# Two tables that fix the issue sequence of five queues in a top-32 attention, FFN and Sinkhorn MoE kernel

## The chip, the cores and the metric

One core of a Trainium2 chip runs the whole program. The metric is device time in microseconds; a kernel's time is the median of its runs. The engines are PE (TensorE, matrix products and transposes), DVE (VectorE), ACT (ScalarE), POOL (GpSimd) and SP (SyncE, whose queue issues the DMAs). Each engine works through one queue of its own in the order in which the program lists its instructions, and waits on semaphores for the others.

## The reference

All data are float32. Attention takes q, k, v of 2 batches x 8 heads x 576 positions x 64; then come a dense FFN and a mixture of 8 experts that are all evaluated for all 1152 tokens.

```python
scores = scale * np.matmul(q, k.transpose(0, 1, 3, 2))
kth = np.partition(scores, -top_k, axis=-1)[..., -top_k:-top_k + 1]   # top_k = 32
scores = np.where(scores >= kth, scores, -1e9)
attn = np.exp(scores - np.max(scores, axis=-1, keepdims=True))
attn = attn / (np.sum(attn, axis=-1, keepdims=True) + 1e-09)
x = np.matmul(attn, v)                        # put together to 1152 x 512
h = x @ w_in                                  # 512 x 2048
x = (h * (1.0 / (1.0 + np.exp(-h)))) @ w_out  # 2048 x 512
logits = x @ w_gate
P = np.exp(logits - logits.max())             # 1152 x 8
for _ in range(8):
    P /= P.sum(1, keepdims=True) + 1e-09
    P /= P.sum(0, keepdims=True) + 1e-09
    P *= N / E
for e in range(E):                            # w1[e] 512 x 1024, w2[e] 1024 x 512
    out += P[:, e:e + 1] * (np.maximum(x @ w1[e], 0.0) @ w2[e])
```

## The kernel before

Most products are split: each operand becomes a high and a low part in the format fp32r, and `mm3` (L145 to L147) issues three matmuls for one. `split` (L135, L136) and `evac_split` (L139, L140) make the parts: ACT copies the high part, and POOL or DVE subtracts.

**Attention** (to about 500 us) goes in five groups g = 0 to 4 of query rows, over four head pairs each. `score_tile` handles a tile of 128 rows x 576 columns: PE makes the scores (L320), ACT copies them to `s` (L323), and DVE finds the 32 largest of each row in four rounds: a MAX (L333) takes the next eight into `m8`, and between two rounds a MATCH_REPLACE (L340) strikes these eight out, writing the copy `w`, which the next MAX reads. ACT has meanwhile made the exponentials `e`; one SCALAR_TENSOR_TENSOR (L343) masks them with the 32nd largest value and sums the row, a RECIPROCAL (L346) follows, ACT scales the tile (L348), PE transposes it (L351, L354) and multiplies it by v (`av`, L370). So the seven MAX and MATCH_REPLACE of one tile and its L343 each need the result of the one ahead. There are 64 such tiles, with up to three of them under way on DVE at a time.

**Beside it** PE gets other work: the first token tile's FFN (`first_row`), experts for that tile (`row_ffn`, with `gr_e` on ACT at L658), and the FFN of group g (`m1` to `m4`, names `g_m`, `gH_m`, `gL_m`) once the group's attention `xH`, `xL` is there. From 500 us on come `m4`, expert 0 for the last four token tiles (`e0_5`), and, in between, the gate logits and six of the eight Sinkhorn iterations (`iteration`, L912 to L921): in each of them DVE makes column sums `cs` (L917), PE adds them over the partitions with a small matmul `pm_c` (L906), and DVE goes on from its result. From about 644 us on experts 7 to 1 follow (products `h`, `yA`, `yB`), in which PE works almost without a break.

**What sets the order.** The program is traced in source order; a scheduler then sorts each engine's instructions by priorities (`tc.cur_priority`, set all over the kernel) and by its own estimate of when they could run, with a few hand-written constraints (`tc.issue_after`). Buffers of a pool are shared by tiles with the same tag, in the order in which the schedule comes to the tiles.

## Time and profile before

| | |
|---|---|
| time, median of 3 runs | 1222.95 us (1221.66 to 1225.37) |
| profiled execution | 1223.69 us, span 1221.8 us |
| busy: PE, DVE, ACT, POOL | 1180.3, 799.5, 611.2, 584.2 us |
| from 12 to 500 us: PE, DVE | 462.1 and 473.7 us of 488 |

The busy time of an engine counts its instructions on the chip; what is missing to the stretch is idle time. In lists of instructions the first number is the start in us from the beginning of the span and the second the length of one instruction (or of several alike, xN). An engine is pipelined, so a next instruction may start shortly before the one ahead has ended; the distance between two starts is what an instruction costs its queue. Buffer and tile numbers are left out in the trace's names; the rows of the queues below have them.

### The profile page before, as it was taken

To read this page: it belongs to the slowest core of one execution; us is meant where nothing else is said; L and a number is where in the kernel's file an instruction comes from. 1 tells how busy PE (TensorE), PEld (TensorE's weight loads), DVE (VectorE), ACT (ScalarE), POOL (GpSimd) and SP (SyncE) were. 2 spreads that over 40 slices of the span, in tenths; PEclk is the share of its full clock that TensorE was granted. 3 is DMA by queue.
4 is the path that set the end of the run, shared out by engine and by line. 5 is a ranking of instruction groups with operands and counts; after the bars stand their busy time and mean duration, and the time that the engine had idled before them with its cause. 6 is when DMAs were issued, how large, how long until landed. Compare 5 with 4: busy or idle time off the path is not lost.

```text
span 1221.8 us, 18254 instructions
## 1 busy us (share of the span) xinstructions
PE 1180.3 (97%) x6278; PEld 961.8 (79%) x6278; DVE 799.5 (65%) x1543; ACT 611.2 (50%) x1243; POOL 584.2 (48%) x662
## 2 busy tenths in 40 slices
...
DVE  7989999999999999203557624634445345344444
...
GB/s 275 278 317 333 278 234 288 301 316 274 253 261 235 270 332 287 279 325 370 293 57 129 77 79 35 52 74 48 52 52 38 84 35 35 70 51 52 18 1 69
DMA packets 131725, 210.94 MB, mean 173 GB/s; under 512 B 23472, under 2 KB 69552, under 8 KB 131632
## 3 DMA queue, kind: packets, MB, share of 16 engines
...
## 4 chain that ended last, share of the span: by engine, by line
PE 80%; DVE 10%; DMA 4%; ACT 2%; issue 2%; POOL 1%; SPq 0%; POOLq 0%; DVEq 0%; ACTq 0%
PE h L145 9%; PE h L146 9%; PE h L147 9%; PE bank L145 5%; PE bank L147 5%; PE bank L146 4%; PE yA L147 4%; PE yB L147 4%; PE yB L145 4%; PE yA L145 4%; PE yA L146 4%; PE yB L146 4%; PE bank L647 4%; DVE m L333 3%; PE pav L370 3%; DVE w L340 3%
## 5 line engine op out<-in xcount | busy, mean ns | idle before, releaser
L136 POOL TENSOR_TENSOR wp<-rw,wp 128x512 fp32r<-128x512 f32 (+1 forms) x56 | 86.6, 1565 | 194.8 <-ACT wp L135 194.8
L333 DVE MAX8 m<-w 128x8 f32<-128x576 f32 x192 | 139.7, 745 | 0.5
L136 POOL TENSOR_TENSOR wa<-raw,wa 128x512 fp32r<-128x512 f32 x88 | 116.2, 1333 | 35.7 <-ACT wa L135 23.9
L136 POOL TENSOR_TENSOR w<-rw,w 128x512 fp32r<-128x512 f32 x56 | 72.3, 1296 | 91.4 <-ACT w L135 91.4
L340 DVE MATCH_REPLACE8 w<-m,w 128x576 f32<-128x576 f32 x128 | 94.4, 740 | 0.0
L145 PE MATMUL yB<-w,gH_0b 128*128 128x512 f32 x208 | 80.9, 389 | 0.0
L146 PE MATMUL yB<-w,gH_0b 128*128 128x512 f32 x208 | 80.9, 389 | 0.0
L1042 DVE SCALAR_TENSOR_TENSOR gL_0b<-gB,gH_0b 128x512 fp32r<-128x512 f32 (+1 forms) x56 | 43.8, 784 | 55.7 <-ACT gH_0b L1041 54.9
L147 PE MATMUL yB<-w,gL_0b 128*128 128x512 f32 x208 | 80.1, 389 | 0.0
L1041 ACT ACTIVATE gH_0b<-gB 128x512 fp32r<-128x512 f32 (+1 forms) x56 | 33.6, 599 | 76.2 <-PE yB L146 43.5
L145 PE MATMUL h<-x1H,wp 128*128 128x512 f32 x168 | 66.1, 393 | 0.0
L146 PE MATMUL h<-x1L,wp 128*128 128x512 f32 x168 | 65.8, 392 | 0.0
L147 PE MATMUL h<-x1H,wp 128*128 128x512 f32 x168 | 65.8, 392 | 0.0
L343 DVE SCALAR_TENSOR_TENSOR s<-s,m,e 128x576 f32<-128x576 f32 x64 | 63.4, 990 | 0.6
L1055 DVE TENSOR_TENSOR gB<-u,h 128x512 f32<-128x512 f32 x56 | 38.5, 687 | 35.6 <-PE h L147 35.5
L135 ACT ACTIVATE wa<-raw 128x512 fp32r<-128x512 f32 x88 | 54.9, 638 | 9.8 <-DMA raw<-in_moe_w_dram 6.5
L135 ACT ACTIVATE w<-rw 128x512 fp32r<-128x512 f32 x56 | 34.6, 626 | 49.2 <-PE yB L147 48.3
L647 PE MATMUL bank<-wb,gT_e 128*128 128x512 f32 x128 | 57.7, 594 | 0.6 <-ACT gT_e L666 0.6
L145 PE MATMUL bank<-xH,wa 128*128 128x256 f32 x192 | 56.9, 296 | 1.2 <-DVE g_m L463 1.2
L338 ACT ACTIVATE e<-s,sm 128x576 f32<-128x576 f32 x64 | 50.2, 784 | 12.9 <-DVE s L343 6.9
L136 DVE TENSOR_TENSOR wp<-sp,wp 128x1024 fp32r<-128x1024 f32 x28 | 45.3, 1617 | 15.3 <-ACT wp L135 15.3
L348 ACT ACTIVATE s<-s,sm 128x576 f32<-128x576 f32 x64 | 50.0, 783 | 9.3 <-DVE sm L346 9.0
...
## 6 DMA issues: line engine op xcount, KB each, us to landing
...
```

The costliest lines, as they stand in the source:

```text
L135: nc.scalar.activation(dH, src, AF.Copy)
L136: eng.tensor_sub(dL, src, dH.bitcast(F32))
L145: nc.tensor.matmul(ps, wH, xH, start=first, stop=False, skip_group_check=more)
L146: nc.tensor.matmul(ps, wH, xL, start=False, stop=False, skip_group_check=more)
L147: return nc.tensor.matmul(ps, wL, xH, start=False, stop=last, skip_group_check=more)
L333: nc.vector.max(mr, src)
L338: nc.scalar.activation(e, s, AF.Exp, scale=SCALE, bias=sm[:, 0:1])
L340: nc.vector.match_replace(out=w, in_to_replace=mr, in_values=src, imm_value=-3e38)
L343: masked.append(nc.vector.scalar_tensor_tensor(s, s, m8[:, TOPK - 1 : TOPK], e, op0=ALU.is_ge, op1=ALU.mult, accum_out=sm[:, 1:2]))
L348: nc.scalar.activation(s, s, AF.Copy, scale=sm[:, 3:4])
L647: seconds.append(nc.tensor.matmul(y, gT[:, c * P : (c + 1) * P], b[c], start=F == 0 and c == 0, stop=F == nF - 1 and c == NDC - 1))
L1042: nc.vector.scalar_tensor_tensor(gL, src, 0.0, gH.bitcast(F32), op0=ALU.max, op1=ALU.subtract)
```

## The change

The five engines are wrapped, so that each instruction issued through them is noted in a list per queue, in the sequence of the source. At the end of the kernel `issue_in` reads the table `ISSUE`, in which the instructions of each queue stand as numbers of that list, and ties each to the one ahead of it by a constraint that only the scheduler sees (no semaphore on the chip). The table `TILES` ties twelve pairs of instructions of different queues, such that tiles with a shared tag get their buffers in a set sequence. No instruction is added, removed or altered on any engine.

```diff
+ISSUE = {
+    "tensor": """
+0-6 19-22 7-10 28-29 11 30 12-13 31 14-18 59-60 47-50 61-62 51-54 68-71 55-58 99-100 23-27 87-90 101-102 91-94
...
+TILES = [
...
+    ("scalar", "vector", """
+403:386 403:467 403:374 403:427 403:345 403:415 403:456 810:697 810:772 810:735
+"""),
...
+class Queue:
+
+    def __init__(self, engine):
+        self.engine, self.traced = engine, []
...
+    def __getattr__(self, name):
+        make = getattr(self.engine, name)
...
+        def call(*args, **kw):
+            ins = make(*args, **kw)
+            self.traced.append(ins.ins)
+            return ins
+        return call
...
+class Queues:
...
+    def issue_in(self, tc, order, tiles):
...
+        behind = mybir.DependencyInfo(mybir.DependencyClass.NoSync, mybir.DependencyReason.SCHED_ONLY)
+        for name, text in order.items():
+            places = []
+            for run in text.split():
+                a, _, b = run.partition("-")
+                places.extend(range(int(a), int(b or a) + 1))
+            traced = getattr(self, name).traced
+            for a, b in zip(places, places[1:]):
+                tc.add_manual_dep(traced[b], traced[a].name, behind, reason="order of the queue")
+        for first, then, text in tiles:
+            for pair in text.split():
+                a, b = (getattr(self, q).traced[int(i)] for q, i in zip((first, then), pair.split(":")))
+                tc.add_manual_dep(b, a.name, behind, reason="order of a tag's tiles")
...
-    nc = tc.nc
+    nc = Queues(tc.nc)
...
-    make_identity(nc, ident)
+    make_identity(tc.nc, ident)
...
+    nc.issue_in(tc, ISSUE, TILES)
```

All engines keep their sets of instructions, and the shifts are local (PE by up to some 45 places, and 77 for the first of the `pm_c`; DVE by about ten); from expert 6 on the sequences are the same. In the changed kernel every instruction bears L341, the line of the wrapper, so it is to be followed by its tiles.

The first place is DVE in group 3 of the attention, head pair 1 of batch 1 (tiles `3_1_1_0_1`, `3_1_1_1_0`, `3_1_1_1_1` are three score tiles; the last number counts buffers). Before:

```order
L333 MAX m8_3_1_1_1_0_5413<-w_3_1_1_1_0_5412 128x8
L333 MAX m8_3_1_1_1_1_5446<-s_3_1_1_1_1_5443 128x8
L333 MAX m8_3_1_1_0_1_5380<-w_3_1_1_0_1_5379 128x8
L340 MATCH_REPLACE w_3_1_1_1_0_5412<-m8_3_1_1_1_0_5413,w_3_1_1_1_0_5412 128x576
L343 SCALAR_TENSOR_TENSOR s_3_1_1_0_1_5377,sm_3_1_1_0_1_5381<-s_3_1_1_0_1_5377,m8_3_1_1_0_1_5380,e_3_1_1_0_1_5382 128x576
L340 MATCH_REPLACE w_3_1_1_1_1_5445<-m8_3_1_1_1_1_5446,s_3_1_1_1_1_5443 128x576
L333 MAX m8_3_1_1_1_0_5413<-w_3_1_1_1_0_5412 128x8
L346 RECIPROCAL sm_3_1_1_0_1_5381<-sm_3_1_1_0_1_5381 128x1
L333 MAX m8_3_1_1_1_1_5446<-w_3_1_1_1_1_5445 128x8
L340 MATCH_REPLACE w_3_1_1_1_0_5412<-m8_3_1_1_1_0_5413,w_3_1_1_1_0_5412 128x576
L340 MATCH_REPLACE w_3_1_1_1_1_5445<-m8_3_1_1_1_1_5446,w_3_1_1_1_1_5445 128x576
L333 MAX m8_3_1_2_0_0_5507<-s_3_1_2_0_0_5504 128x8
```

And in the changed kernel:

```order
L341 MAX m8_3_1_1_0_1_5380<-w_3_1_1_0_1_5379 128x8
L341 MATCH_REPLACE w_3_1_1_0_1_5379<-m8_3_1_1_0_1_5380,w_3_1_1_0_1_5379 128x576
L341 TENSOR_TENSOR qL_1_3_0_5494<-pq_1_3_0_5488,qq_1_3_0_5493 128x512
L341 RECIPROCAL sm_3_1_1_0_0_5348<-sm_3_1_1_0_0_5348 128x1
L341 MAX m8_3_1_1_1_1_5446<-s_3_1_1_1_1_5443 128x8
L341 MAX m8_3_1_1_0_1_5380<-w_3_1_1_0_1_5379 128x8
L341 MAX m8_3_1_1_1_0_5413<-w_3_1_1_1_0_5412 128x8
L341 SCALAR_TENSOR_TENSOR s_3_1_1_0_1_5377,sm_3_1_1_0_1_5381<-s_3_1_1_0_1_5377,m8_3_1_1_0_1_5380,e_3_1_1_0_1_5382 128x576
L341 MATCH_REPLACE w_3_1_1_1_0_5412<-m8_3_1_1_1_0_5413,w_3_1_1_1_0_5412 128x576
L341 MAX m8_3_1_1_1_0_5413<-w_3_1_1_1_0_5412 128x8
L341 MATCH_REPLACE w_3_1_1_1_0_5412<-m8_3_1_1_1_0_5413,w_3_1_1_1_0_5412 128x576
L341 RECIPROCAL sm_3_1_1_0_1_5381<-sm_3_1_1_0_1_5381 128x1
```

Before, instructions of different tiles take turns, and none of these twelve directly follows one whose result it needs; now three do: the MATCH_REPLACE of tile `3_1_1_0_1`, and a MAX and a MATCH_REPLACE of tile `3_1_1_1_0`. Over the whole attention the direct followers of the same tile go from 13 to 53 where a MATCH_REPLACE follows its MAX, from 18 to 60 where a MAX follows its MATCH_REPLACE, and from 6 to 26 where the L343 of a tile follows its last MAX.

The second place is DVE where the sequence before already has such neighbours, at tile `1_0_3_0_1` in group 1:

```order
L333 MAX m8_1_0_3_0_0_2191<-w_1_0_3_0_0_2190 128x8
L343 SCALAR_TENSOR_TENSOR s_1_0_3_0_0_2188,sm_1_0_3_0_0_2192<-s_1_0_3_0_0_2188,m8_1_0_3_0_0_2191,e_1_0_3_0_0_2193 128x576
L333 MAX m8_1_0_3_0_1_2224<-s_1_0_3_0_1_2221 128x8
L340 MATCH_REPLACE w_1_0_3_0_1_2223<-m8_1_0_3_0_1_2224,s_1_0_3_0_1_2221 128x576
L346 RECIPROCAL sm_1_0_3_0_0_2192<-sm_1_0_3_0_0_2192 128x1
L333 MAX m8_1_0_3_0_1_2224<-w_1_0_3_0_1_2223 128x8
L340 MATCH_REPLACE w_1_0_3_0_1_2223<-m8_1_0_3_0_1_2224,w_1_0_3_0_1_2223 128x576
L333 MAX m8_1_0_3_0_1_2224<-w_1_0_3_0_1_2223 128x8
L340 MATCH_REPLACE w_1_0_3_0_1_2223<-m8_1_0_3_0_1_2224,w_1_0_3_0_1_2223 128x576
L333 MAX m8_1_0_3_0_1_2224<-w_1_0_3_0_1_2223 128x8
L333 MAX m8_1_0_3_1_0_2257<-s_1_0_3_1_0_2254 128x8
L343 SCALAR_TENSOR_TENSOR s_1_0_3_0_1_2221,sm_1_0_3_0_1_2225<-s_1_0_3_0_1_2221,m8_1_0_3_0_1_2224,e_1_0_3_0_1_2226 128x576
```

And in the changed kernel:

```order
L341 MAX m8_1_0_3_0_0_2191<-w_1_0_3_0_0_2190 128x8
L341 MATCH_REPLACE w_1_0_3_0_0_2190<-m8_1_0_3_0_0_2191,w_1_0_3_0_0_2190 128x576
L341 MAX m8_1_0_3_0_0_2191<-w_1_0_3_0_0_2190 128x8
L341 RECIPROCAL sm_1_0_2_1_1_2120<-sm_1_0_2_1_1_2120 128x1
L341 MAX m8_1_0_3_0_1_2224<-s_1_0_3_0_1_2221 128x8
L341 SCALAR_TENSOR_TENSOR s_1_0_3_0_0_2188,sm_1_0_3_0_0_2192<-s_1_0_3_0_0_2188,m8_1_0_3_0_0_2191,e_1_0_3_0_0_2193 128x576
L341 MATCH_REPLACE w_1_0_3_0_1_2223<-m8_1_0_3_0_1_2224,s_1_0_3_0_1_2221 128x576
L341 MAX m8_1_0_3_0_1_2224<-w_1_0_3_0_1_2223 128x8
L341 MATCH_REPLACE w_1_0_3_0_1_2223<-m8_1_0_3_0_1_2224,w_1_0_3_0_1_2223 128x576
L341 MAX m8_1_0_3_0_1_2224<-w_1_0_3_0_1_2223 128x8
L341 RECIPROCAL sm_1_0_3_0_0_2192<-sm_1_0_3_0_0_2192 128x1
L341 MAX m8_1_0_3_1_0_2257<-s_1_0_3_1_0_2254 128x8
```

Here the MATCH_REPLACE and MAX of tile `1_0_3_0_1` follow each other in both kernels; a MAX of another tile and a RECIPROCAL have moved in between them.

The third place is PE at the last two of the six column sums `pm_c`, at the end of expert 0's four token tiles (`bank` and `y4` are its outputs). Before:

```order
L147 MATMUL y4_0_7049<-wb_512_7921,gL_e0_5_7_7938 128x512
L147 MATMUL y4_1_7050<-wb_512_7921,gL_e0_5_7_7938 128x512
L906 MATMUL pm_c4_7704<-cs_4_7701,ones_63 128x8
L906 MATMUL pm_c5_7717<-cs_5_7714,ones_63 128x8
L145 MATMUL h_7_0_0_8137<-x1H_1040,wp_7_0_8035 128x512
L146 MATMUL h_7_0_0_8137<-x1L_1041,wp_7_0_8035 128x512
```

And in the changed kernel:

```order
L341 MATMUL pm_c4_7704<-cs_4_7701,ones_63 128x8
L341 MATMUL y4_0_7049<-wb_509_7888,gL_e0_5_6_7905 128x512
L341 MATMUL bank0_132<-wb_512_7921,gH_e0_5_7_7937 128x512
L341 MATMUL y4_1_7050<-wb_512_7921,gH_e0_5_7_7937 128x512
L341 MATMUL bank1_133<-wb_512_7921,gH_e0_5_7_7937 128x512
L341 MATMUL y4_0_7049<-wb_512_7921,gH_e0_5_7_7937 128x512
L341 MATMUL y4_1_7050<-wb_512_7921,gL_e0_5_7_7938 128x512
L341 MATMUL y4_0_7049<-wb_512_7921,gH_e0_5_7_7937 128x512
L341 MATMUL bank1_133<-wb_512_7921,gL_e0_5_7_7938 128x512
L341 MATMUL y4_0_7049<-wb_512_7921,gL_e0_5_7_7938 128x512
L341 MATMUL pm_c5_7717<-cs_5_7714,ones_63 128x8
L341 MATMUL bank0_132<-wb_512_7921,gL_e0_5_7_7938 128x512
```

The fifth `pm_c` has moved up past products of `e0_5`, so that nine of them now stand between it and the sixth, where there was none.

## Rows read from the trace of the kernel before

**Rows 1.** The page: busy time, DVE in 40 slices, and the chain.

```profile
PE 1180.3 (97%) x6278; PEld 961.8 (79%) x6278; DVE 799.5 (65%) x1543; ACT 611.2 (50%) x1243; POOL 584.2 (48%) x662
...
DVE  7989999999999999203557624634445345344444
...
PE 80%; DVE 10%; DMA 4%; ACT 2%; issue 2%; POOL 1%; SPq 0%; POOLq 0%; DVEq 0%; ACTq 0%
```

**Rows 2.** Stretches of the span: busy time of each engine (x instructions), clock.

```profile
core 0: us, PE busy (x) PEld busy (x) DVE busy (x) ACT busy (x) POOL busy (x), PEclk, DMA share, GB/s
...
12.00:500.00 488.00, 462.10 (x2936) 366.96 (x2936) 473.72 (x1051) 381.60 (x814) 294.63 (x377) 1.00 0.85 286
500.00:660.00 160.00, 155.08 (x867) 129.45 (x865) 60.56 (x131) 59.65 (x140) 64.86 (x67) 0.99 0.69 244
660.00:1222.00 562.00, 557.79 (x2461) 461.53 (x2460) 261.50 (x353) 164.25 (x281) 218.31 (x203) 1.00 0.18 53
```

**Rows 3.** Waits of DVE from 12 to 500 us: total, times, longest.

```profile
DVE sm L346 <- POOL sm L345: 2.6, 5, 0.7
...
DVE g_m L463 <- ACT t_m L461: 0.2, 1, 0.2
```

**Rows 4.** Waits of PE, 12 to 500 us, first and last of 21.

```profile
PE ps L320 <- ACT s L323: 4.1, 4, 2.8
...
PE bank L145 <- ACT gH_m L135: 0.2, 1, 0.2
```

**Rows 5.** DVE in order of time, 160 to 178 us: start, length, instruction.

```profile
167.57 0.76 DVE L333 MAX8 m<-w 128x8 f32<-128x576 f32 x1
168.44 1.66 DVE L343 SCALAR_TENSOR_TENSOR s<-s,m,e 128x576 f32<-128x576 f32 x1
...
172.54 0.74 DVE L340 MATCH_REPLACE8 w<-m,w 128x576 f32<-128x576 f32 x1
173.32 0.76 DVE L333 MAX8 m<-w 128x8 f32<-128x576 f32 x1
...
174.19 0.74 DVE L340 MATCH_REPLACE8 w<-m,w 128x576 f32<-128x576 f32 x1
...
175.65 0.74 DVE L333 MAX8 m<-s 128x8 f32<-128x576 f32 x1
176.31 0.80 DVE L343 SCALAR_TENSOR_TENSOR s<-s,m,e 128x576 f32<-128x576 f32 x1
```

**Rows 6.** DVE in order of time, 336 to 352 us.

```profile
339.65 0.73 DVE L333 MAX8 m<-w 128x8 f32<-128x576 f32 x1
...
340.37 0.73 DVE L340 MATCH_REPLACE8 w<-m,w 128x576 f32<-128x576 f32 x1
...
341.83 0.73 DVE L340 MATCH_REPLACE8 w<-m,s 128x576 f32<-128x576 f32 x1
342.49 0.74 DVE L333 MAX8 m<-w 128x8 f32<-128x576 f32 x1
```

**Rows 7.** All engines at the end of the attention, 497.6 to 500 us.

```profile
497.71 0.78 ACT L348 ACTIVATE s<-s,sm 128x576 f32<-128x576 f32 x1
...
499.81 0.38 PE L351 MATMUL pt<-ident,s 128*128 128x128 f32 x2
```

**Rows 8.** All engines around the sixth column sum, 641 to 649 us.

```profile
641.62 0.28 PE L906 MATMUL pm_c<-cs,ones 128*128 128x8 f32 x2
...
643.98 0.46 PE L906 MATMUL pm_c<-cs,ones 128*128 128x8 f32 x2 [2.07 <-DVE cs L917]
...
644.29 0.78 PE L145 MATMUL h<-x1H,wp 128*128 128x512 f32 x1
...
647.42 0.47 PE L146 MATMUL h<-t2L,wp 128*128 128x512 f32 x1
...
647.96 0.40 PE L145 MATMUL h<-t2H,wp 128*128 128x512 f32 x1
...
648.19 0.39 PE L146 MATMUL h<-t2L,wp 128*128 128x512 f32 x1
```

250 lines of the change are left out of this document (added), and 7 rows, old and new, of the table ISSUE.

## The prediction

> **What bounds the kernel now.** I read the page first: PE is busy for 1180.3 of 1221.8 us, the chain that ended last lies on PE for 80% of its length and on DVE for 10% [rows 1]. A reader could stop there and say that only PE counts. The 40 slices show why not: DVE's digits are 7 to 9 in the first sixteen slices (30.5 us each) and 0 to 7 after that, so the kernel has two stages. The stretches put numbers to it. From 12 to 500 us DVE is busy for 473.7 of 488 us and PE for 462.1; from 660 us on PE has 557.8 of 562 and DVE 261.5 [rows 2]. So in the attention stage the queue with the least room is DVE's, with 14.3 us idle against 25.9 us on PE, and behind 660 us nothing but PE's own work matters. The waits agree: in the same stretch DVE's seven kinds of wait sum to 9.5 us, from 2.6 us down to 0.2 [rows 3], and PE's 21 kinds to 25.9 us, from 4.1 down to 0.2 [rows 4]. The largest of PE's is a score matmul that waits for a copy of `s`, the tile which DVE works on; the stages hang on each other in both directions.
>
> How do the two meet at the end of the attention? The last tile is scaled on ACT until 497.71 + 0.78 = 498.49 us, and PE takes it up for its transposes at 499.81 [rows 7]. PE was thus 1.3 us behind DVE's chain there. A delay of that chain by more than 1.3 us stops PE at this place of its queue, with all that is queued behind it: the last `av`, then `m4`, expert 0, and the experts.
>
> **The change, part by part.** No instruction is added or removed, and no semaphore. What can change is the distance between starts on a queue, and waits.
>
> *DVE's neighbours.* The rows of DVE's queue printed with the change say which instructions belong to one tile. At tile `1_0_3_0_1` a MATCH_REPLACE starts at 172.54, the MAX on its result at 173.32, and the next MATCH_REPLACE, on that MAX, at 174.19: distances 0.78 and 0.87 us [rows 5]. In the first place shown of the queue before, where tiles take turns, MAX to the MATCH_REPLACE of another tile is 340.37 - 339.65 = 0.72, and MATCH_REPLACE to the MAX of another 342.49 - 341.83 = 0.66 [rows 6]. From the last MAX of a tile to its own L343 it is 168.44 - 167.57 = 0.87 (tile `1_0_3_0_0`), and to the L343 of another tile 176.31 - 175.65 = 0.66 [rows 5]. No wait is recorded at any of these starts, and the operands have the same shape. So a DVE instruction that needs the result of the one directly ahead starts later by 0.15, 0.12 and 0.21 us; the turns of the order before hide exactly this. The change has 40, 42 and 20 more such neighbours: 40 x 0.15 + 42 x 0.12 + 20 x 0.21 = 6.0 + 5.0 + 4.2 = **+15.2 us** of DVE's time, all of it before 500 us. Bounds: 0 if these late starts had another cause, 15.2 in full.
>
> Against this stands a rule of the Trainium skill: "VectorE: DVE Perf Modes", section "The DRAIN you can't avoid", says that a next DVE instruction waits until the pipeline is empty whatever it depends on, and that chaining without semaphores saves nothing. By it the order of neighbours would be free, and this term 0; the same section adds that some next instructions may start earlier. The trace does not bear the strict form out: at 339.65 a MAX of 0.73 us is followed after 0.72 [rows 6], at 173.32 one of 0.76 us after 0.87 [rows 5].
>
> *DVE's idle time.* The longer chain doesn't all come out at the end, because DVE has gaps into which it can grow. There are 14.3 us from 12 to 500 us [rows 2], of which 9.5 are waits with a known releaser [rows 3] (POOL's `sm`, ACT's `g_m` and `s`, POOL's `cv_n`). A wait on something that comes at a fixed time is used up by delay; a wait on something that is itself late by DVE's delay is not. Bounds 0 and -14.3; I take half of the waits, **-4.8**, as the new order moves about as many DVE instructions towards their inputs as away.
>
> *PE's moves before 500 us.* PE's pieces move by tens of places, the `pav` of the attention keep theirs, and DMA issues on SP change places by about ten. They act on PE's 25.9 us of waits. While DVE is the queue with the least room, a PE stall less brings tiles to DVE earlier only where DVE waited for them, which the last term has already. I take 0; were DVE not the bound, it would be worth up to half of it (a rival below).
>
> *The end of the attention.* PE's 1.3 us [rows 7] absorb as much: **-1.3**.
>
> *The column sums.* Before, PE stands between the fifth and sixth `pm_c` for 2.07 us, and from the fifth at 641.62 to the sixth at 643.98 it is 2.36 us [rows 8], which is the length of DVE's small operations between them. Now nine products stand there; 512 columns cost 648.19 - 647.96 = 0.23 us [rows 8], nine 2.07. Of the wait some 0.3 remains: **-1.8**. Bounds 0, if DVE's chain is kept up, and -2.1.
>
> *The clock behind it.* After that stall the matmuls of 512 columns start 0.45 us apart, from 644.29 to 647.42 seven times, against 0.23 later [rows 8]: TensorE's clock had been at the lower of its two levels, half. Without the stall the fall has no occasion that I see: 7 x 0.22 = **-1.5**, bounds 0 and -1.5.
>
> *Elsewhere* DVE's and ACT's moves after 500 us are small and their queues idle for half of the time or more [rows 2]; from expert 6 on the sequences are the same. 0, hidden behind PE's 155.1 of 160 and 557.8 of 562 us.
>
> The sum is 15.2 - 4.8 - 1.3 - 1.8 - 1.5 = **+5.8 us**. The profiled execution took 1223.69 us, so 1229.5; the median of the runs stands 0.7 below it, which makes **1228.8 us**.
>
> **The rivals.** *PE is the bound after all* (faster). It is busy for 95% of the attention stage and its stalls show in the chain; if DVE's delay is absorbed by tiles that are ready ahead of PE's turn, the new sequence only removes PE's waits. Half of 25.9 us and the 3.3 of the column sums give 1222.95 - 13 - 3.3 = 1206.7; a quarter 1213. For it: PE's waits in that stage are nearly three times DVE's, and all that follows stands in PE's queue. Against: the 1.3 us at the last tile [rows 7], where DVE's chain must be less than 1.3 us late for this to hold, which takes 13.9 of DVE's 14.3 idle us. Chance 0.26.
>
> *Neighbours cost nothing* (faster), the mechanism being that the late starts of rows 5 come from something else than the result ahead. Then -4.8 - 3.3 = -8.1, 1215. The distances repeat too evenly for me: 0.07.
>
> *The terms cancel* (no change): DVE wins back 10 us or more of its idle time, 15.2 - 10.5 - 1.3 - 3.3 = 0.1, 1223. The tables could also have no effect, but the queues printed above differ as they say. 0.17.
>
> *The whole delay arrives* (slower by more): no idle time is regained, and the column sums give nothing since DVE's chain there runs against PE as before: 15.2 - 1.3 = +13.9, 1236.8; new waits of ACT behind late L343 could add to it. 0.14.
>
> **How the numbers follow.** The forecast has 0.36. The three runs before span 0.3%, 3.7 us, and a difference below that can't be told from none. Faster: 0.26 + 0.07 = 0.33. Same: 0.17. Slower: 0.36 + 0.14 = 0.50. The range goes from the PE case with nearly half of its waits gone, 1208, to the whole delay with some 2 us of new waits, 1239. The slower cases alone would be 1227 to 1239.
>
> **What would show it.** Right: in the changed profile DVE's busy time from 12 to 500 us grows little, or its gaps between same-tile starts stay at 0.78 to 0.87; the last L343 of the attention ends 8 to 12 us later than 497; PE's transposes L351 wait more for ACT's scaled `s`; the wait at the sixth `pm_c` is below 0.6 us and no stretch at half clock stands behind it. Wrong: the last L343 ends at 497 or sooner. Then either the price of a neighbour is not what rows 5 and 6 say, or the idle time of DVE was not waiting for fixed times but for PE. It would also be wrong, with the mechanism right, if PE regained what DVE loses through work that the new sequence puts into the wait at the last tiles.

## The result and the profile after

The changed kernel takes 1239.24 us (median of 4 runs, 1237.81 to 1242.65) against 1223.0 us before (median of 4, one run more than above): a ratio of 1.0135, with a 95% interval of 1.0109 to 1.0161. It is slower by 16.2 us where +5.8 was forecast, and 0.2 us above the upper end of the range, less than the runs differ among themselves. The profiled execution took 1242.65 us, with a span of 1240.9 us, so the differences below add up to the 19.1 us between the two spans and stand some 3 us above those of the medians.

The page of the changed kernel, three rows that answer to [rows 1]:

```profile
PE 1191.6 (96%) x6278; PEld 964.7 (78%) x6278; DVE 805.6 (65%) x1543; ACT 611.8 (49%) x1243; POOL 575.2 (46%) x662
...
DVE  7989999999999999402365634534534445344444
...
PE 66%; DVE 25%; DMA 3%; ACT 3%; issue 1%; SPq 1%; ACTq 0%; POOL 0%; DVEq 0%
```

DVE's busy sum rises by 6.1 us and PE's by 11.3. What moves most is the chain that ended last: DVE had 10% of it and now has 25%. The attention is held by DVE to a larger part than before. The stretches of [rows 2], in the changed kernel:

```profile
12.00:500.00 488.00, 455.21 (x2818) 355.60 (x2819) 472.98 (x1025) 368.83 (x781) 280.32 (x366) 0.99 0.81 275
500.00:660.00 160.00, 155.31 (x905) 129.84 (x904) 55.95 (x126) 62.31 (x152) 58.55 (x68) 0.99 0.74 264
```

DVE is as busy as before in the 488 us (473.0 us) but has done 26 instructions fewer in them (1025 instead of 1051); PE has done 118 fewer. So the same work takes longer, and it is not a stretch of idle time that shows it. The distances between starts do. Here is DVE's queue at the second place that the change shows (tile `1_0_3_0_1`), in order of time:

```profile
179.01 0.74 DVE L341 MAX8 m<-s 128x8 f32<-128x576 f32 x1
179.67 0.80 DVE L341 SCALAR_TENSOR_TENSOR s<-s,m,e 128x576 f32<-128x576 f32 x1
...
180.47 0.74 DVE L341 MATCH_REPLACE8 w<-m,s 128x576 f32<-128x576 f32 x1
181.25 0.76 DVE L341 MAX8 m<-w 128x8 f32<-128x576 f32 x1
...
182.12 0.75 DVE L341 MATCH_REPLACE8 w<-m,w 128x576 f32<-128x576 f32 x1
```

A MAX and the L343 of another tile stand 0.66 us apart; MATCH_REPLACE and the MAX of its own tile 0.78, that MAX and the next MATCH_REPLACE 0.87. These are the distances of [rows 5, 6], and there are 102 such neighbours more.

The waits of DVE and of PE from 12 to 514 us (in all, times, longest), which answer to [rows 3, 4]:

```profile
DVE g_m L341 <- ACT g_m L341: 4.7, 2, 4.5
DVE m L341 <- ACT s L341: 1.3, 5, 0.4
...
PE pq L341 <- ACT kk L341: 4.1, 2, 2.1
PE pt L341 <- DVE xL L341: 3.5, 3, 2.5
PE pk L341 <- ACT kk L341: 3.0, 3, 1.3
PE pt L341 <- ACT s L341: 2.9, 2, 1.8
```

DVE's waits sum to 9.3 us in eight kinds; before it was 9.5 in seven. In sum none was given back, though the kinds changed: the waits of `sm` for POOL went from 2.6 to 0.3 us, and one on `g_m` has grown. PE's sum to 33.7 us; over the attention before (12 to 500 us) it was 25.9. At the end of the attention:

```profile
510.58 0.82 DVE L341 SCALAR_TENSOR_TENSOR s<-s,m,e 128x576 f32<-128x576 f32 x1
...
512.88 0.78 ACT L341 ACTIVATE s<-s,sm 128x576 f32<-128x576 f32 x1
...
517.88 0.49 PE L341 MATMUL pt<-ident,s 128*128 128x128 f32 x3
```

The last L343 ends at 511.4 us, where it ended at 497.2. PE takes up its tile 4.2 us after ACT's scaling has ended (513.66), where it was 1.3 [rows 7]. So PE has become late by more than DVE's chain is. (The sequence of PE also decides where this tile stands among its other work, so the 4.2 us are not all lateness.) The place of the column sums:

```profile
660.83 0.28 PE L341 MATMUL pm_c<-cs,ones 128*128 128x8 f32 x2
660.96 0.48 PE L341 MATMUL y<-wb,gL_e 128*128 128x512 f32 x1
...
663.19 0.39 PE L341 MATMUL pm_c<-cs,ones 128*128 128x8 f32 x2
...
663.75 0.39 PE L341 MATMUL h<-x1H,wp 128*128 128x512 f32 x1
663.98 0.39 PE L341 MATMUL h<-t2H,wp 128*128 128x512 f32 x1
```

The fifth and sixth `pm_c` are still 2.36 us apart, but products fill the time: no wait, and behind it the products stand 0.23 apart at once, where they stood 0.45 apart [rows 8].

One more place is new. It shows PE, DVE and ACT around 437 us:

```profile
433.09 1.84 DVE L341 SCALAR_TENSOR_TENSOR s<-s,m,e 128x576 f32<-128x576 f32 x1
...
436.44 0.41 DVE L341 TENSOR_TENSOR xL<-pav,xH 128x256 fp32r<-128x256 f32 x1
...
435.03 0.78 ACT L341 ACTIVATE e<-s,sm 128x576 f32<-128x576 f32 x1 [3.31 <-DVE s L341]
436.56 0.78 ACT L341 ACTIVATE s<-s,sm 128x576 f32<-128x576 f32 x1 [0.75 <-DVE sm L341]
437.24 0.36 ACT L341 ACTIVATE g_e<-bank 128x256 f32<-128x256 f32 x1
...
436.90 0.33 PE L341 MATMUL pt<-ident,s 128*128 128x128 f32 x1 [2.46 <-DVE xL L341]
437.66 0.58 PE L341 MATMUL bank<-x1H,wa 128*128 128x256 f32 x1 [0.43 <-ACT g_e L341]
```

DVE makes the low part `xL_3` only at 436.44, eight places behind the point at which its input is there, and PE's transpose waits for it. ACT's `e` waits for an L343, and behind `e` in ACT's queue stands `g_e`, on which PE's next product waits.

**Where the 19.1 us lie.** I compared, in both traces, when PE has done the same amount of work, and added up the distances of all DVE starts up to the last L343. DVE's chain is 14.2 us later at its end: neighbours +13.3 (their distances beyond 0.72, 0.66 and 0.66 us, which is what the same pairs take without the result directly ahead), and +0.9 in small pieces of both signs. DVE's gaps are none of it: those of more than 0.2 us from 12 us to the last L343 are 8.9 us before and 8.8 now. PE is 18.9 us behind at that work, 4.7 more than DVE's chain. From there to the column sums it loses 2.6 more (one wait for a transfer, `wa`, went from 0.7 to 1.8 us; the rest is small pieces), and at the column sums it regains 2.7. That makes 18.8; 0.3 is left. The split between 4.7 and 2.6 is not sharp: the two sequences differ there, and by the point chosen between 500 and 530 us PE is 16.8 to 19.0 us behind.

The pages divide the same 19.1 us another way: 11.3 us are busy time of PE, and the rest is its idle time. The lower clock, which is granted more often now, makes at most 3.4 of the 11.3 (see "Why the prediction was off"). Some 8 us are left in which PE waits for nothing and its work itself takes longer, as far as the profile's modelled ends of matmuls can tell. They go with PE's sequence: PE's busy sum is 1185.5 to 1195.4 us in the five kernels below that have the sequence of the change on PE (the changed one, e1, e12, e17, e18), and 1178.3 to 1184.1 in the seven that have that of before, all or nearly all of it (before, e2, e3, e4, e9, e11, e16). For e1 and e9:

```profile
PE 1189.1 (96%) x6278; PEld 962.3 (78%) x6278; DVE 796.4 (64%) x1543; ACT 613.3 (50%) x1243; POOL 574.3 (46%) x662
```

```profile
PE 1184.1 (96%) x6278; PEld 963.8 (78%) x6278; DVE 804.4 (65%) x1543; ACT 609.7 (49%) x1243; POOL 575.7 (46%) x662
```

What in the sequence makes PE's work longer was not found.

### The profile page after: what moved, and what is told of

It is laid out like the page before. It is cut to its first block, busy times and chain, and to the rows that moved or that the text cites. A ratio compares the mean times of both kernels' runs of the same rounds, so it can differ in the third digit from the quotient of the medians.

```text
span 1240.9 us, 18215 instructions
## 1 busy us (share of the span) xinstructions
PE 1191.6 (96%) x6278; PEld 964.7 (78%) x6278; DVE 805.6 (65%) x1543; ACT 611.8 (49%) x1243; POOL 575.2 (46%) x662
## 4 chain that ended last, share of the span: by engine, by line
PE 66%; DVE 25%; DMA 3%; ACT 3%; issue 1%; SPq 1%; ACTq 0%; POOL 0%; DVEq 0%
PE h L341 25%; PE yA L341 12%; PE yB L341 12%; PE bank L341 10%; DVE m L341 9%; DVE w L341 8%; DVE s L341 3%; PE y L341 2%; PE pav L341 1%; PE pt L341 1%; DVE m_h L341 1%; DMA wfr<-in_moe_w_in_dram 1%; DVE w_h L341 1%; PE ps L341 1%; DVE s_h L341 1%
## 5 line engine op out<-in xcount | busy, mean ns | idle before, releaser
L341 POOL TENSOR_TENSOR wp<-rw,wp 128x512 fp32r<-128x512 f32 (+1 forms) x56 | 86.5, 1566 | 189.8 <-ACT wp L341 189.8
L341 DVE MAX8 m<-w 128x8 f32<-128x576 f32 x192 | 141.4, 752 | 1.8
L341 POOL TENSOR_TENSOR wa<-raw,wa 128x512 fp32r<-128x512 f32 x88 | 113.4, 1300 | 33.6 <-ACT wa L341 21.6
L341 PE MATMUL yB<-w,gH_0b 128*128 128x512 f32 x416 | 127.2, 389 | 0.0
L341 PE MATMUL h<-x1H,wp 128*128 128x512 f32 x336 | 117.9, 389 | 0.5 <-ACT p L341 0.5
L341 POOL TENSOR_TENSOR w<-rw,w 128x512 fp32r<-128x512 f32 x56 | 72.5, 1298 | 88.9 <-ACT w L341 88.9
L341 DVE MATCH_REPLACE8 w<-m,w 128x576 f32<-128x576 f32 x128 | 94.9, 743 | 0.0
L341 PEld LDWEIGHTS yB<-w,gH_0b 128*128 128x128 f32 x416 | 78.1, 188 | 16.2
L341 PE MATMUL bank<-xH,wa 128*128 128x256 f32 x384 | 87.7, 294 | 1.3 <-DVE g_m L341 1.0
L341 DVE SCALAR_TENSOR_TENSOR gL_0b<-gB,gH_0b 128x512 fp32r<-128x512 f32 (+1 forms) x56 | 44.5, 795 | 55.6 <-ACT gH_0b L341 54.9
L341 PE MATMUL yB<-w,gL_0b 128*128 128x512 f32 x208 | 80.1, 389 | 0.0
L341 PE MATMUL pt<-ident,s 128*128 128x128 f32 x320 | 68.0, 282 | 8.4 <-DVE xL L341 3.5
L341 PEld LDWEIGHTS h<-x1H,wp 128*128 128x128 f32 x336 | 63.1, 188 | 13.9 <-ACT p L341 1.0
L341 PEld LDWEIGHTS bank<-xH,wa 128*128 128x128 f32 x384 | 65.5, 191 | 9.4 <-DVE g_m L341 2.9
L341 ACT ACTIVATE gH_0b<-gB 128x512 fp32r<-128x512 f32 (+1 forms) x56 | 33.6, 600 | 76.2 <-PE yB L341 43.5
L341 PE MATMUL bank<-wb,gH_m 128*128 128x512 f32 x192 | 69.5, 418 | 0.8 <-ACT gH_m L341 0.6
L341 PE MATMUL h<-x1L,wp 128*128 128x512 f32 x168 | 65.2, 389 | 0.0
L341 PE MATMUL bank<-wb,gT_e 128*128 128x512 f32 x128 | 63.3, 594 | 0.2 <-ACT gT_e L341 0.2
L341 DVE SCALAR_TENSOR_TENSOR s<-s,m,e 128x576 f32<-128x576 f32 x64 | 62.3, 974 | 1.5
L341 DVE TENSOR_TENSOR gB<-u,h 128x512 f32<-128x512 f32 x56 | 38.5, 688 | 36.9 <-PE h L341 36.9
L341 ACT ACTIVATE w<-rw 128x512 fp32r<-128x512 f32 x56 | 34.7, 627 | 54.5 <-PE yB L341 48.3
L341 ACT ACTIVATE aT<-pt 128x512 f32<-128x512 f32 (+1 forms) x128 | 54.9, 439 | 12.4 <-PE pt L341 12.1
## 6 DMA issues: line engine op xcount, KB each, us to landing
wa<-sk SPq DMA_DIRECT2D x64, 512.0 KB, 4.6
wb<-sk SPq DMA_DIRECT2D x64, 512.0 KB, 4.9
wb<-in_moe_w_dram SPq DMA_DIRECT2D x32, 512.0 KB, 4.3
sk<-wa SPq DMA_DIRECT2D x24, 512.0 KB, 3.8
sk<-wb SPq DMA_DIRECT2D x24, 512.0 KB, 4.0
wfr<-in_moe_w_in_dram SPq DMA_DIRECT2D x16, 512.0 KB, 5.6
```

The source lines that it names most:

```text
L341: ins = make(*args, **kw)
```

## The experiments

All kernels issue the same instructions; only sequences differ. They are written by tables as in the change (`TILES` has 23 pairs there, not twelve; the kernels that start from the changed one have it, those that start from the kernel before don't). The diffs show rows of a queue in its sequence, without line numbers, at one of the places. "Last L343" is the end of the attention's last one (497.2 us before, 511.4 in the changed kernel). The kernel before was run again beside each group of runs, with medians from 1223.2 to 1224.7 us; the ratios and the differences to before are taken against these.

| run | what | us | ratio to before, 95% |
|---|---|---|---|
| e1_sep | changed kernel, 107 neighbours parted | 1241.59 | 1.0126 to 1.0168 |
| e2_join139 | before, 103 neighbours made | 1230.61 | 1.0042 to 1.0072 |
| e3_join217 | before, 180 neighbours made | 1245.88 | 1.0161 to 1.0195 |
| e4_col | before, `pm_c4` nine products earlier | 1221.59 | 0.9962 to 0.9988 |
| e7_early_b | before to 60 us, then changed | 1235.23 | 1.0089 to 1.0126 |
| e13_from_225 | before to 225 us, then changed | 1230.03 | 1.0036 to 1.0082 |
| e14_from_320 | before to 320 us, then changed | 1231.83 | 1.0051 to 1.0084 |
| e8_late_a | before to 530 us, then changed | 1222.89 | 0.9989 to 1.0008 |
| e9_pe_of_before | changed, PE's sequence of before | 1241.17 | 1.0103 to 1.0158 |
| e10_pe_of_after | before, PE's sequence of changed | 1250.55 | 1.0183 to 1.0231 |
| e11_pe_and_dve | e9 with neighbours parted | 1235.68 | 1.0064 to 1.0118 |
| e12_act_pool_sp | changed, ACT, POOL, SP of before | 1269.16 | 1.0331 to 1.0389 |
| e5_grp_sep | e1 with PE's work grouped by kind | 1267.07 | 1.0351 to 1.0384 |
| e6_shuf | before, PE's work interleaved | 1250.95 | 1.0215 to 1.0245 |
| e15_shuf_r | before, only fp32r products interleaved | 1231.17 | 1.0047 to 1.0092 |
| e17_xl3 | changed, one split earlier | 1240.22 | 1.0114 to 1.0156 |
| e18_sep_xl3 | e1, the same split earlier | 1242.92 | 1.0133 to 1.0184 |
| e16_best | e4 with 9 neighbours parted | 1224.71 | 0.9996 to 1.0018 |

### The price of a neighbour

Three kernels change DVE's sequence alone. In e2 and e3 the queues are those of before, with instructions of one tile moved next to each other (DVE, tile `3_1_1_0_1`, in e2):

```diff
 MAX m8_3_1_1_0_1_5380<-w_3_1_1_0_1_5379 128x8
+SCALAR_TENSOR_TENSOR s_3_1_1_0_1_5377,sm_3_1_1_0_1_5381<-s_3_1_1_0_1_5377,m8_3_1_1_0_1_5380,e_3_1_1_0_1_5382 128x576
 MATCH_REPLACE w_3_1_1_1_0_5412<-m8_3_1_1_1_0_5413,w_3_1_1_1_0_5412 128x576
-SCALAR_TENSOR_TENSOR s_3_1_1_0_1_5377,sm_3_1_1_0_1_5381<-s_3_1_1_0_1_5377,m8_3_1_1_0_1_5380,e_3_1_1_0_1_5382 128x576
```

> The queues of the kernel before, word for word, but for DVE, where in each stretch of 50 instructions MAX, MATCH_REPLACE and L343 are pulled behind the instruction of the same tile that they need, by at most two places, until there are as many such neighbours as the change has there: 140 for 37. Theory N: 26 x 0.15 + 51 x 0.12 + 26 x 0.2 = +15.2 us, 1234 to 1239 us. Rival P: 1221 to 1226 us.

It rose by 6.7 us, and neither range holds. The last L343 came 8.7 us later, of 12.8 us of price in the trace. Of the difference some 3.7 us are two-input instructions that ran shorter; the rest is spread over many rows. e3 goes further (tile `3_1_1_1_0`):

```diff
+MATCH_REPLACE w_3_1_1_1_0_5412<-m8_3_1_1_1_0_5413,w_3_1_1_1_0_5412 128x576
 MAX m8_3_1_1_1_1_5446<-s_3_1_1_1_1_5443 128x8
 MAX m8_3_1_1_0_1_5380<-w_3_1_1_0_1_5379 128x8
-MATCH_REPLACE w_3_1_1_1_0_5412<-m8_3_1_1_1_0_5413,w_3_1_1_1_0_5412 128x576
```

> As the last, with all the neighbours that moves by at most two places can make: 217 for 37. Theory N: 57 x 0.15 + 92 x 0.12 + 31 x 0.2 = +25.8 us, 1243 to 1250 us. Rival P: 1221 to 1227 us. A kernel in which DVE's idle time takes up a part would stand below N by a constant in both doses.

It rose by 21.9 us, with the last L343 22.0 us later, of 23.0 us of price. No other queue was touched, so neighbours on DVE do carry into the time, nearly in full at this dose. PE's waits show where it arrives (12 to 514 us):

```profile
PE pt L274 <- ACT s L274: 8.5, 8, 2.0
PE ps L274 <- ACT s L274: 6.4, 5, 4.8
```

The transposes wait for scaled tiles, as the prediction described. Then the other way round, in e1: the changed kernel, with other instructions put between neighbours (139 of them down to 32):

```diff
 MAX m8_3_1_1_1_0_5413<-w_3_1_1_1_0_5412 128x8
+MATCH_REPLACE w_3_1_1_1_1_5445<-m8_3_1_1_1_1_5446,s_3_1_1_1_1_5443 128x576
 MATCH_REPLACE w_3_1_1_1_0_5412<-m8_3_1_1_1_0_5413,w_3_1_1_1_0_5412 128x576
 RECIPROCAL sm_3_1_1_0_1_5381<-sm_3_1_1_0_1_5381 128x1
-MATCH_REPLACE w_3_1_1_1_1_5445<-m8_3_1_1_1_1_5446,s_3_1_1_1_1_5443 128x576
```

> The changed kernel with DVE's table alone altered: MAX and MATCH_REPLACE of other tiles are moved by at most three places in between, so that direct followers of the same tile on DVE fall from 139 to 32 (37 before the change); the other four queues stay. Theory N (the price of a neighbour arrives in full, since DVE is the bound of the attention): 37 x 0.15 + 47 x 0.12 + 23 x 0.2 = about 15.7 us come back, 1223 to 1227 us, and the last L343 ends 13 to 16 us sooner than at 511.4. Rival P (PE's moved instructions and their waits make the loss, DVE's longer chain is absorbed): 1236 to 1241 us.

It took 1241.59 us: nothing came back. The price did go (18.6 to 4.5 us), but DVE's gaps went from 8.8 to 22.6 us, and the last L343 still ends at 512.0. DVE's and PE's waits in this run:

```profile
DVE m L342 <- ACT s L342: 11.6, 13, 2.2
...
PE pt L342 <- ACT s L342: 5.3, 4, 1.8
```

DVE now waits 13 times for score tiles. So neighbours are enough to make the kernel slow (e3), but taking them away doesn't make the changed kernel fast. There is a second limit at nearly the same height: the other engines, in their new sequences, don't bring the tiles sooner.

### The column sums

The kernel before, with one PE instruction moved:

```diff
 MATMUL bank1_133<-wb_512_7921,gH_e0_5_7_7937 128x512
+MATMUL pm_c4_7704<-cs_4_7701,ones_63 128x8
 MATMUL bank1_133<-wb_512_7921,gH_e0_5_7_7937 128x512
...
 MATMUL y4_1_7050<-wb_512_7921,gL_e0_5_7_7938 128x512
-MATMUL pm_c4_7704<-cs_4_7701,ones_63 128x8
 MATMUL pm_c5_7717<-cs_5_7714,ones_63 128x8
```

> The queues of the kernel before, but for the fifth pm_c, which PE gets nine products earlier. The prediction's terms for the column sums: -1.8 for the wait and -1.5 for the half clock behind it, 1219 to 1221 us. Rival: the sums' chain on DVE keeps its length and the clock falls anyway, 1222 to 1224 us.

It took 1221.59 us, between the two ranges, and 2.4 us less than the kernel before beside it. In the trace PE gains 3.6 us at this place, with the sum of the two terms forecast at 3.3. Its rows:

```profile
640.83 0.28 PE L276 MATMUL pm_c<-cs,ones 128*128 128x8 f32 x2
...
643.19 0.39 PE L276 MATMUL pm_c<-cs,ones 128*128 128x8 f32 x2
```

This part of the change is right by itself, and a small gain.

### Where along the kernel it is lost

Four kernels take one sequence up to a time and the other after it, on all queues. Shown is the first place of DVE that differs, in e7 against the changed kernel and in e13, e14 and e8 against before:

```diff
+TENSOR_TENSOR kk_0_0_155<-pk_0_0_156,kk_0_0_155 64x512
 TENSOR_TENSOR kk_0_0_155<-bank0_132,kk_0_0_155 64x64
-TENSOR_TENSOR kk_0_0_155<-pk_0_0_156,kk_0_0_155 64x512
```

> The changed kernel, but with the sequence of before on all five queues up to about 60 us. In the profile of the changed kernel PE is 5 us late by then. Theory W: these 5 us come back to the end, 1233 to 1236 us. Theory N+S (what follows is bound by DVE's neighbours and PE's changes of kind, each by itself): DVE was 6 us late there as well, so most of it comes back too, 1233 to 1237 us; if later slack had absorbed it, 1238 to 1241.

The median is 4.0 us below the changed kernel's, but against the kernels before beside them the two ratios overlap (1.0089 to 1.0126 and 1.0109 to 1.0161). In the trace, which is of the slowest of e7's four runs (1238.96 us), the last L343 still ends at 511.3 us and DVE waits 6.1 us for a `g_m`. So that the first 60 us hold 4 us of the loss is not shown.

```diff
+MATCH_REPLACE w_2_0_1_1_0_3488<-m8_2_0_1_1_0_3489,w_2_0_1_1_0_3488 128x576
+SCALAR_TENSOR_TENSOR g_m1_0_2356<-t_m1_0_2357,bank2_134 128x256
+MAX m8_2_0_1_1_0_3489<-w_2_0_1_1_0_3488 128x8
 MATCH_REPLACE w_2_0_1_0_0_3455<-m8_2_0_1_0_0_3456,w_2_0_1_0_0_3455 128x576
-SCALAR_TENSOR_TENSOR g_m1_0_2356<-t_m1_0_2357,bank2_134 128x256
```

> The sequences of before on all five queues up to about 225 us, those of the change from there on. Theory D (the loss is spread over the attention as DVE's neighbours are, 15.2 us of them by 500 us and 7 of these before 225): 1229 to 1233 us. Rival E (the loss stands in the first stretches, before 225 us, where the changed profile shows 7.5 us of its delay and e7_early_b gave back 4): what is left is below that, 1224 to 1228 us. Rival F (it stands behind 225 us): 1235 to 1241 us.

+6.5 us, as a loss spread over the attention has it.

```diff
+RECIPROCAL sm_3_1_0_0_0_5188<-sm_3_1_0_0_0_5188 128x1
+MAX m8_3_1_0_1_1_5286<-w_3_1_0_1_1_5285 128x8
+MATCH_REPLACE w_3_1_0_1_1_5285<-m8_3_1_0_1_1_5286,w_3_1_0_1_1_5285 128x576
 MAX m8_3_1_0_1_0_5253<-w_3_1_0_1_0_5252 128x8
-RECIPROCAL sm_3_1_0_0_0_5188<-sm_3_1_0_0_0_5188 128x1
```

> The same with the seam at about 320 us; 8 of the 15.2 us of DVE's neighbours stand behind it, as do 6 to 7 of the 19 us of delay in the changed profile, less the 3 that the column sums give back. Theory D: 1225 to 1229 us. If the loss behind 225 us is that of the stretch from 225 to 285 us alone, where PE falls back by 5.5 us: 1221 to 1224 us.

+8.3 us, more than expected, and not less than from 225 us on. Its DVE waits 4.6 us for one `g_m` at 79 us, where before waits 1.9 and e13 1.0 with the same sequence up to there. This wait differs between profiles of one sequence, so e13 and e14 can't be told apart. In both PE falls 3 us behind around 418 to 433 us and 2 to 3 us from 458 to 509 us, beyond DVE's delay.

```diff
 SCALAR_TENSOR_TENSOR g_m4_6_7260<-t_m4_6_7261,h_454_7245 128x256
+TENSOR_TENSOR gL_m4_6_7259<-g_m4_6_7260,gH_m4_6_7258 128x256
 TENSOR_REDUCE mxe_71<-lt_4_6971 8x1
-TENSOR_TENSOR gL_m4_6_7259<-g_m4_6_7260,gH_m4_6_7258 128x256
```

> The queues of before up to about 530 us, and those of the change from there on. The column sums and the clock give -2 to -3.5 (e4_col: -2.4); the changed kernel's trace showed PE losing some 2.5 us between 530 and 620 us to two waits for DMA, which either belong to its sequence (then 1222 to 1224 us) or come from the earlier part (then 1219 to 1221).

No change: in the trace the column sums give 2.6 us, and PE falls 2 us behind between 530 and 580 us. Recorded waits for transfers are only a part of that (1.3 us from 530 to 660 us, 0.7 before). So the whole of the 16 us net lies ahead of 530 us, and by e13 and e14 some 6 to 8 of it behind 225 or 320 us.

### Is it one queue?

e9 gives the changed kernel PE's sequence of before (in 142 of the 147 stretches in which they differ); the first places:

```diff
-MATMUL pk_0_1_1_199<-ident_58,kn_0_1_145 128x128
+MATMUL ps_0_0_0_1_0_253<-kk_0_0_155,qL_0_0_0_175 128x288
 MATMUL ps_0_0_0_1_0_253<-kk_0_0_155,qL_0_0_0_175 128x288
...
-MATMUL ps_0_0_0_1_0_253<-kk_0_0_155,qL_0_0_0_175 128x288
+MATMUL pk_0_1_1_199<-ident_58,kn_0_1_145 128x128
```

> The changed kernel with PE's sequence put back: in 142 of the 147 stretches in which the two sequences differ (2656 of 2747 instructions) PE has the sequence of before; DVE, ACT, POOL and SP keep that of the change, DVE its 139 neighbours. Theory P (PE's sequence makes the loss; DVE's neighbours cost what e2_join139 showed alone, +7 us, and are hidden behind PE's loss): 1228 to 1232 us. Rival Q (the sequences of ACT, POOL and SP make it): 1236 to 1241 us.

1241.17 us, just above rival Q. PE's busy sum falls by 7.5 us (row in the section on the result), but its idle time grows by 5.7, and the time stays. So PE's sequence alone is not the second limit. e10 is the reverse, on the kernel before (135 of 147 stretches), and the same places turn round:

```diff
-MATMUL ps_0_0_0_1_0_253<-kk_0_0_155,qL_0_0_0_175 128x288
+MATMUL pk_0_1_1_199<-ident_58,kn_0_1_145 128x128
 MATMUL ps_0_0_0_1_0_253<-kk_0_0_155,qL_0_0_0_175 128x288
```

> The kernel before with PE's sequence of the change in 135 of the 147 stretches (2391 of 2747 instructions); the other four queues, DVE's 37 neighbours among them, as before. Theory P: PE's sequence alone makes most of the loss, 1234 to 1242 us. Rival Q: 1221 to 1227 us.

1250.55 us, worse than either kernel whole; DVE's gaps are 32.2 us. e11 is e9 with DVE's edit of e1:

```diff
 MAX m8_3_1_1_1_0_5413<-w_3_1_1_1_0_5412 128x8
+MATCH_REPLACE w_3_1_1_1_1_5445<-m8_3_1_1_1_1_5446,s_3_1_1_1_1_5443 128x576
 MATCH_REPLACE w_3_1_1_1_0_5412<-m8_3_1_1_1_0_5413,w_3_1_1_1_0_5412 128x576
```

> The changed kernel with both: PE's sequence of before as in e9, and DVE's neighbours separated as in e1_sep. With e1, e9 and the changed kernel itself it makes a square. Theory P with hidden neighbours: 1222 to 1227 us, that is, taking the neighbours away is worth some 5 us here, where it was worth nothing with PE's new sequence. Rival Q: 1235 to 1241 us.

1235.68 us, in the range of rival Q; and yet, as theory P had it, with PE's sequence of before the neighbours are worth 5.5 us (against e9), and without it they were worth none (e1). So the two limits do stand beside each other. Eleven us stay. e12 gives the changed kernel the sequences of before on ACT, POOL and SP (169 of 205 stretches); ACT's first place:

```diff
+ACTIVATE kk_0_0_155<-bank0_132 64x64
 ACTIVATE s_0_0_0_0_0_225<-ps_0_0_0_0_0_220 128x576
-ACTIVATE kk_0_0_155<-bank0_132 64x64
```

> The changed kernel with ACT, POOL and SP put back to the sequence of before in 169 of 205 stretches (751 of 1034 instructions); PE and DVE as in the change. Theory P: 1235 to 1242 us. Rival Q: 1223 to 1230 us.

1269.16 us, with 35.0 us of gaps on DVE. In e10 and e12 queues taken over from the other kernel cost more than they bring, and in e9 one brings nothing; sequences that fit each other would explain it. Such a swap can't say how much of the loss belongs to a queue.

### PE's changes of kind

In the changed kernel PE goes more often from one kind of work to another (1301 times instead of 565). e5 takes e1 and groups PE's work (675 changes):

```diff
-MATMUL ps_1_0_1_1_1_1950<-kk_0_1_188,qq_0_1_1_1685 128x288
-MATMUL bank1_133<-ident_58,gr_e0_1_1136 128x128
 MATMUL bank2_134<-wa_33_1179,x1H_1040 128x512
...
+MATMUL ps_1_0_1_1_1_1950<-kk_0_1_188,qq_0_1_1_1685 128x288
```

> The changed kernel with DVE's neighbours separated as in e1_sep, and PE's table regrouped: instructions are pulled forward by at most five places behind one of the same kind (transpose or product, type, columns), none is put back by more than six, so that changes of kind on PE fall from 1301 to 675 (565 before the change). Theory S (each change of kind on PE costs some 14 ns, which a fit of PE's pace over the runs so far gives, and PE is co-bound): 626 x 0.014 = 8.8 us less than e1_sep, 1231 to 1235 us. Rival W (PE's loss is its waits for data that the sequence asks for too soon, above all in the first 60 us): 1238 to 1243 us.

1267.07 us; both theories missed. Grouping made score tiles late: DVE's wait for them is now the largest, 19.9 us in 15 times. e6 goes the other way and interleaves PE's work in the kernel before (1193 changes):

```diff
+MATMUL bank0_132<-wb_26_1120,gT_e0_1_1146 128x512
 MATMUL pt_1_0_0_1_0_1781<-ident_58,s_1_0_0_1_0_1762 128x128
+MATMUL bank0_132<-wb_26_1120,gT_e0_1_1146 128x512
 MATMUL pt_1_0_0_1_0_1781<-ident_58,s_1_0_0_1_0_1762 128x128
```

> The queues of the kernel before but for PE, whose instructions from about 90 us on are pulled forward by at most eight places, so that changes of kind rise from 565 to 1193; DVE keeps its 37 neighbours. Theory S: 628 x 0.014 = +8.8 us, 1229 to 1234 us. Rival W: a move by a few places is within the slack, 1222 to 1226 us.

1250.95 us, beyond the expectation, again with late inputs of DVE (13.6 us for `xL`). Neither run separates a price of changing from late products, so e15 interleaves only the products in fp32r, at places where nothing waits for them soon (1306 changes):

```diff
+MATMUL ps_2_0_2_1_0_3710<-kk_0_2_308,qq_0_2_3_3584 128x288
 MATMUL bank2_134<-xH_1_1674,wa_174_2436 128x256
+MATMUL ps_2_0_2_1_0_3710<-kk_0_2_308,qq_0_2_3_3584 128x288
```

> The queues of before, but PE's fp32r products of 512, 288 and 256 columns are interleaved among themselves by at most eight places, which leaves every transpose and every fp32 product where it was: changes of kind go from 565 to 1306, more than in e6_shuf. Theory S (a change of kind by itself costs 14 to 18 ns): +10 to +13 us, 1233 to 1237 us. Rival R (e6_shuf lost by its broken fp32 pairs and by transposes that came late, and a change of kind costs nothing): 1222 to 1227 us.

1231.17 us, in neither range, but not by the changes: up to 446 us PE is not behind before by more than 0.5 us, with some 350 changes more, and its waits up to there are 26.4 us against 25.9, so no price is hidden in them. From 551 to 640 us, where PE hardly waits, some 170 changes more add nothing either. It loses some 8 us from 446 to 551 us, where its waits for ACT's late `gH_m` and `g_m` sum to 5.9 us. A change of kind among these products costs nothing that can be seen in the first and the last of these stretches.

### One wait of PE

The largest new wait is that of 2.46 us at 436.90 (shown above). e17 moves the split it waits for, in the changed kernel:

```diff
 MATCH_REPLACE w_4_1_0_1_0_6414<-m8_4_1_0_1_0_6415,w_4_1_0_1_0_6414 128x576
+TENSOR_TENSOR xL_3_5163<-pav_3_1_3_5791,xH_3_5162 128x256
 MAX m8_4_1_0_1_1_6448<-w_4_1_0_1_1_6447 128x8
...
-TENSOR_TENSOR xL_3_5163<-pav_3_1_3_5791,xH_3_5162 128x256
```

> The changed kernel with one DVE instruction moved: the low part of xL_3 from pav_3_1_3 stands eight places earlier, so that it can run at about 430.2 us, right behind ACT's high part, and not at 436.44. The product of all else stays. Theory W (PE is late on its own account, by single waits like this one): the transpose at 436.90 no longer waits 2.46 us and no half clock stands behind it; the time falls by these 2.5 + 1.5 us to 1234.5 to 1237. Theory B (DVE's chain and PE's work bind at the same height, so that taking one off leaves the other): the wait goes but DVE's last L343 still ends at 511 to 512 and the time falls by less than 1.5 us, 1238 to 1240.

1240.22 us, no gain. The row that waits next:

```profile
437.93 0.38 PE L341 MATMUL bank<-x1H,wa 128*128 128x256 f32 x1 [3.45 <-ACT g_e L341]
```

The transpose no longer waits, and the product behind it does, until nearly the same moment (437.93 us, 437.66 in the changed kernel). ACT's `g_e` stands behind an `e` that waits 3.66 us for an L343. The wait named `xL`; with `xL` there in time, the next in line holds PE, and that is again DVE's chain, through ACT. Theory B holds here: the last L343 ends at 511.9 us. e18 makes the same move in e1:

```diff
+TENSOR_TENSOR xL_3_5163<-pav_3_1_3_5791,xH_3_5162 128x256
 MAX m8_4_1_0_1_1_6448<-w_4_1_0_1_1_6447 128x8
```

> The kernel with DVE's neighbours taken apart (32 same-tile neighbours instead of 139) with the same move of xL_3: both limits are lowered at this place. The run with neighbours taken apart alone stood at 1241.6. Theory W: the wait of 1.5 us and the half clock behind it go, 1237.5 to 1239.5. Theory B: with DVE's chain lower by neighbours and PE's wait gone, more comes out than the wait itself, 1231 to 1236, and the last L343 ends at 504 to 508 us.

1242.92 us, the last L343 at 511.6. Both expectations missed: to part the neighbours and to take this wait away frees nothing either, because the same `g_e` holds PE for 2.97 us here.

### A better version

e16 is e4 with nine of the neighbours of before parted on DVE:

```diff
+MAX m8_1_0_3_0_1_2224<-s_1_0_3_0_1_2221 128x8
 MAX m8_1_0_3_0_0_2191<-w_1_0_3_0_0_2190 128x8
+MATCH_REPLACE w_1_0_3_0_1_2223<-m8_1_0_3_0_1_2224,s_1_0_3_0_1_2221 128x576
 SCALAR_TENSOR_TENSOR s_1_0_3_0_0_2188,sm_1_0_3_0_0_2192<-s_1_0_3_0_0_2188,m8_1_0_3_0_0_2191,e_1_0_3_0_0_2193 128x576
```

> The kernel before with the fifth pm_c nine products earlier as in e4_col, and nine of DVE's 37 neighbours separated (28 left). Sum of e4_col's -2.4 and at most 4 x 0.15 + 3 x 0.12 + 2 x 0.2 = 1.4 us of DVE: 1219 to 1222 us; if separated neighbours only bring waits, as in e1_sep, 1221 to 1223.

1224.71 us, above both ranges and no better than before: DVE's gaps grew to 16.6 us. Of all runs only e4 is faster than before, by 0.25%.

## Why the prediction was off

| term | forecast | in the traces |
|---|---|---|
| same-tile neighbours | +15.2 | +13.3 |
| DVE's idle time, and other changes of its chain | -4.8 | +0.9 |
| end of the attention, with PE's moves | -1.3 | +4.7 |
| elsewhere, 515 to 640 us | 0 | +2.6 |
| column sums with the clock behind them | -3.3 | -2.7 |
| sum | +5.8 | +18.8 |

- **The neighbours** were sized nearly right. The median distances in the changed kernel are 0.86, 0.78 and 0.80 us for the three kinds with the result directly ahead, and 0.73, 0.66 and 0.67 without; the L343's price is thus nearer 0.14 than 0.21 us. e3 shows that the sum arrives. The prediction says that no wait is recorded at these starts; the printed rows show none, but the trace's records do. All 139 neighbours of the changed kernel wait for a semaphore that each DVE instruction raises at its end, and start 0.03 us after the end of the one ahead (median); the same pairs of instructions without the result directly ahead start 0.08 us before it. So the price is that of waiting for the end of the one ahead instead of overlapping with it. The strict rule of the Trainium skill ("VectorE: DVE Perf Modes", section "The DRAIN you can't avoid") that the next instruction waits for an empty pipeline is not borne out here: by it e3 would have left the time as it was. The section's own exception, that a next instruction which isn't held starts earlier, agrees with the 0.08 us.
- **The column sums and the clock** were right: no wait at the sixth `pm_c` and no half clock behind it (the granted clock was 0.57 from 644 to 648 us, row below, and is 1.00 from 660 to 667 us in the changed kernel), 2.4 to 3.6 us.

```profile
644.00:648.00 4.00, 4.00 (x12) 3.24 (x13) 3.24 (x8) 2.04 (x5) 4.00 (x4) 0.57 0.30 87
```

- **The step that failed first** is "I take half of the waits, **-4.8**". Nothing was regained in sum: 8.9 us of gaps before, 8.8 after. The argument was that waits on something with a fixed time are used up by delay. Some were (POOL's `sm`, 2.6 to 0.3 us), but others came, and the term had no place for those. The largest wait now is 4.5 us on one `g_m` from 81 to 86 us. With the sequence of the changed kernel there, four profiles show 4.5 to 5.3 us (in two of them DVE's neighbours are parted); with that of before, seven show 0.9 to 4.7. The waits on ACT's `s`, `xH` and `qq` are on work that itself follows DVE.
- **The step that failed most** is "PE's moves before 500 us", where it says "I take 0", with the 1.3 us of slack at the end. PE did not absorb a delay; it became 4.7 us later than DVE's chain. Its waits in the attention grew by 7.8 us. A lower clock is granted in stretches between 40 and 60, 100 and 120, 430 and 450, and 540 and 560 us, where before had two (50 to 60 and 640 to 650); summed over the granted clock this is 6.8 us of clock missing instead of 3.4. And some 8 us of PE's busy time are neither. "Local" shifts were taken as free in a queue whose waits were 25.9 us, with no bound on the side of a loss.
- **The signs.** The distances, the column sums and the clock came as named. The last L343 came 14.2 us later instead of 8 to 12, and PE's waits of `pt` for ACT's `s` went only from 2.5 to 2.9 us: the path that the prediction described is plain in e3, not in the changed kernel.
- **The rivals.** "The whole delay arrives", 1236.8 us with a chance of 0.14, came nearest, and with the addition made there: ACT's `e` at 435.03 does wait 3.31 us behind a late L343, and PE behind ACT. Its other half did not hold, since the column sums did give their part; that the number fits so well is in part luck. "PE is the bound after all" is refuted in its sign: the new sequence adds to PE's waits and to its work. "Neighbours cost nothing" is refuted by e3, and by e2 in part.
- **What stays open.** Why PE, ACT and DVE together are late by nearly as much when the neighbours are parted (e1). No single queue put back gave it back (e9, e12), though such a swap brings new waits and so doesn't clear a queue. It is no change of kind among fp32r products (e15), and not the largest single wait (e17, e18). Why PE's work itself is longer in its new sequence is open too, and so is what `TILES` does by itself, which no run tried. That the sequences of the queues fit each other, so that many small waits close in a ring, agrees with all of these runs; it is argued from them, not shown.
